# One backward-pass kernel: transposes issued one at a time, the order of the last convolution slices, and where the convolution ends

## The chip, the cores and the metric

The kernel runs on one core of a Trainium2 chip. The metric is the device time of one launch in microseconds (us); lower is better. The engines that matter here are TensorE (PE in the profile, with PEld for its weight loads), VectorE (DVE), ScalarE (ACT), GpSimd (POOL, which also issues DMAs) and SyncE (SP, whose queue issues most DMA loads). Each engine runs its instructions in the order in which they were built; engines wait for one another through semaphores.

## The reference

The kernel computes a forward pass and all its gradients. With `x` of 2048 rows and 1024 columns and `xn` its layer norm:

```python
s = A_ref(xn, k, v, shift_k, ssm_k, ssm_D)        # gated long convolution
g = silu(((xn @ w_gate) * (xn @ w_up)) @ w_down)  # bilinear unit, F = 3584
out = x + s * g

def A_ref(q, k, v, shift_k, ssm_k, ssm_D):
    kv = short_conv(k, shift_k, 4 taps) * v
    y = irfft(rfft(kv padded to 4096) * rfft(ssm_k padded))[:2048]
    return q * (y + kv * ssm_D)
```

The outputs are `out` and the gradients of x, k, v, the two convolution kernels, `ssm_D` and the three weights, for a given `grad_out`.

## The kernel before

The sequence is held as 16 row blocks of 128 rows. The first part of the kernel, on which the change works, is this:

- **Gate and up products.** F is cut into 14 slabs of 256 columns (`NSL`). A unit (`gu_unit`, L656) is one slab times four row blocks: per row block eight 128x512 matmuls into a tile `psg` (L671), then a ScalarE copy into `gut` (L673). When a unit's last row block is copied, VectorE multiplies the two halves into `hN` (`multiply`), and TensorE later transposes `hN` in four transposes of 32-bit pairs into a tile `tr` (`turn`, through `turn_pairs`, L205). ScalarE copies `tr` into `hT` (L699), which goes to DRAM (`HTd`). `defer` and `flush` put the transposes some row blocks later in the program; `flush()` without an age puts all that are left at once. The last two slabs are run half by half: first both slabs over row blocks 0 to 7, then both over 8 to 15. Between the halves stands `hn[0](); flush()` (L976 to L978), which puts the multiply and the four transposes of the newest unit right there.
- **The long convolution** (`conv_forward`, L709) runs beside these products. It works in eight slices of 128 columns. Per slice it transforms the kernel row (`h`, loaded, transposed by `h_rows`, then matmuls `psF` L242, ScalarE copies `SP`, VectorE sums into `KX`) and `kv` (into `HX`), multiplies the spectra (`product`), and takes the inverse: VectorE sums (`inv_dft` or `inv8`) followed by matmuls into `psY` in `tail`. `inv8`, with eight residues, makes VectorE do more sums and needs 16 `psY` matmuls (`inv8_rows`, L445); `inv_dft`, with four, needs 32 (`inv_rows`, L456). `INV8` lists the slices that take `inv8`: 2, 4 and 6. Slices 0 and 7 use a forward transform of eight residues (`EIGHT`).
- **Pacing.** The convolution is a generator whose yields give estimated VectorE time. `tick` (L941), called after each row block, advances it by `pump` in proportion to the rows done out of `NT` = 206. VectorE's instructions keep the program's order while `PIN` is set.
- **The down product.** `bm_mm` (L992) multiplies `HTd` rows by `w_down`: 56 matmuls of 128x512 per row block (L994). `bm_first` does row blocks 0 and 1 while the convolution's rest is ticked in; `drain()` puts what is left of the convolution. Then `gate` (L1212) treats each row block: four loads (`x_t`, `do_t`, `xn_t`, `yf_t`, two buffers each; `yf_t` is the convolution's stored result `YFd`), a ScalarE copy of the PSUM tile into `bm`, two sigmoids and eleven VectorE operations. The `w_down` factor's other operand `ht` is loaded for two row blocks at a time (`load_ht`): `ht1` and `ht2` early, the others from the row loop. All these loads go through SP's queue in its built order.

After that come the backward products, with the backward convolution on VectorE beside them; the change leaves them as they are.

Of the kernel before, what the change touches and what calls it, by code (L numbers as in the profile page):

```python
# [13 lines left out]
BF16 = mybir.dt.bfloat16  # L14
# [5 lines left out]
def build_kernel(  # L20
# [12 lines left out]
    P = 128  # L33
# [530 lines left out]
    def in_pairs(x):  # L564
        return x.bitcast(F32).rearrange("p (m q) -> p q m", q=4)

    def turn_row(i, x, q, qi):
        ps = ps_st.tile([P, 4, P], F32, name="tr")
        for dc in range(4):
            tr_ln[0] = turn_pairs(ps[:, dc, :], in_pairs(x)[:, dc])  # L570
        to = by_pair(XNT[q][:, :, qi * P:(qi + 1) * P])
        if i % 2 == 0:
            act_copy[0] = nc.scalar.copy(out=to, in_=halves_of(ps[:]))
        else:
            V.tensor_copy(to, halves_of(ps[:]))

    def layer_norm(b0, n, x4):
# [50 lines left out]
        c, r0 = divmod(b0, 8)  # L628
        return last, root, st(xnn[:, c, r0:r0 + n, :], x4[:, 0:n, :])

    def turn_late():
        for i, (x, q, qi) in enumerate(turn_rows):
            turn_row(i, x, q, qi)
        turn_rows.clear()

    nop = lambda: None
# [7 lines left out]
    def flush(age=0):  # L644

        for e in later:
            e[0] += 1
        while later and later[0][0] >= age:
            later.pop(0)[1]()

    turn_of = [0]
    hn = [nop]
    chunk = [0]

    def gu_unit(sl, b0, n, w, tick):

        if n == 4:
            turn_of[0] += 1
            if turn_of[0] % 3 == 0 and sl < NSL - 2:
                gut = U[5][:, 2048:4096].rearrange("p (a i f) -> p a i f", a=2, i=4)  # L660
            else:
                gut = fg.tile([P, 2, 4, SLW], BF16, name="gut")
            hN = fg.tile([P, 4, SLW], BF16, name="hN", bufs=3)
        else:
            gut = lnp.tile([P, 2, 2, SLW], BF16, name="gut_s", bufs=6)
            hN = lnp.tile([P, 2, SLW], BF16, name="hN_s", bufs=6)
        for i in range(n):
            q, qi = divmod(b0 + i, 4)
            ps = ps_gu.tile([P, 512], F32, name="psg")
            for dc in range(DC):  # L670
                gu_mm[0] = nc.tensor.matmul(ps[:], XNT[q][:, dc, qi * P:(qi + 1) * P],  # L671
                                            w[:, dc].rearrange("p a f -> p (a f)"), start=(dc == 0), stop=(dc == DC - 1))
            nc.scalar.copy(out=gut[:, :, i], in_=ps[:].rearrange("p (a f) -> p a f", a=2))  # L673
            flush(5)
            if i == 0:
                turn_late()
            hn[0]()
            hn[0] = nop
            tick()
        sta(GUd[sl, b0 // 8][:, :, b0 % 8:b0 % 8 + n], gut[:, :, 0:n])  # L680

        def multiply():
            with tc.issue_after(last.ins) if b0 + n <= 4 and chunk[0] <= 2 else nullcontext():
                tt(hN[:, 0:n], gut[:, 0, 0:n], gut[:, 1, 0:n], MUL)
            st(Hd[sl][:, b0:b0 + n, :], hN[:, 0:n])
            defer(turn)
        hn[0] = multiply

        def store(hT):
            fr, so = sl % 12 * SLW, b0 % 8 * P  # L690
            ld(HTd[b0 // 8][sl // 12][fr:fr + SLW, so:so + n * P].rearrange("(f a) s -> f a s", a=2),
               hT[:, :, 0:n].rearrange("f a i s -> f a (i s)"))

        def turn():
            hT = fg.tile([P, 2, 4, P], BF16, name="hT") if chunk[0] > 5 else lnp.tile([P, 2, 4, P], BF16, name="hT_s", bufs=5)
            ps = ps_tr.tile([P, 4, P], F32, name="tr")
            for i in range(n):
                turn_pairs(ps[:, i, :], hN[:, i, :].bitcast(F32))
            nc.scalar.copy(out=hT[:, :, 0:n].rearrange("f a i s -> f i a s"), in_=halves_of(ps[:, 0:n]))  # L699
            store(hT)  # L700

    h_out = []
    EIGHT = ((0, 0), (0, 1), (7, 0), (7, 1))
    INV8 = (2, 4, 6)
    SHIFT_W = 8 * 2.3

    conv_state = {"forward": True}
# [1 line left out]
    def conv_forward():  # L709
# [34 lines left out]
            yield 2.3  # L744

        def h_rows(ds, c):
            if ds == 8:
                return
# [8 lines left out]
            for r in range(1, 4):  # L757
                turn_pairs(ps[:, r, :], pairs[:, c, :, r])
# [66 lines left out]
        h_rows(0, 1)  # L825
        yield 0.1
        tl = turn_tables(ps_y)
        sp = [half(0, S_["hx"], i, Dz[:, 0:P]) for i in range(2)]
        for ds in range(8):
            yield 0.5  # L830
            if ds % 2 == 1 and ds < 7:
                with tc.issue_after(S_["kst"].ins):
                    for c in range(2):
                        load_kv(ds // 2 + 1, c)
            D0 = Dz[:, ds * P:(ds + 1) * P]
            sph = []
            KX = cx.tile([P, 16, 256], BF16, name="KX")
            HX = cs.tile([P, 16, 256], BF16, name="HX", bufs=2)
            own_room = lambda X: X[:].rearrange("p a x -> p (a x)").bitcast(F32).rearrange("p (a x) -> p a x", a=8)[:, 0:4]
            eight = (ds, 1) in EIGHT  # L840
            if ds == 0:
                yield from transform(0, 1, sp, HX, own_room(KX), lambda i: sph.append(half(0, kvs(0), i)), nop)
            else:
                yield from transform(ds, 0, sp, KX, own_room(HX), lambda i: sph.append(half(ds, S_["hx"], i, D0)), nop)
                S_["kst"] = st(KFd[ds], KX[:])
            next(tl, None)
            room = cf.tile([P, 4, 256], F32, name="room", tag="hx")[:] if eight else None
            yield from transform(ds, int(ds > 0), sph, HX if ds else KX, room, nop1 if eight else lambda c: h_rows(ds + 1, c),
                                 lambda: next(tl, None))
            if ds == 0:  # L850
                S_["kst"] = st(KFd[0], KX[:])
            if eight:
                h_rows(ds + 1, 0)
            turned(HX, 1, 0, 1)
            yield 1.3
            if eight:
                h_rows(ds + 1, 1)
            if ds == 7:
                cf.release()
                S_["forward"] = False  # L860
            st(HFd[ds], HX[:])
            yield from product(KX, HX, KX, cs, False, 0)
            if ds % 2 == 1 and ds < 7:
                yield from shift(ds // 2 + 1)
            sp = []

            def ahead():
                if ds < 7:
                    sp.append(half(ds + 1, kvs(ds + 1), len(sp)))
            yield from (inv8 if ds in INV8 else inv_dft)(KX, HX, cs, ahead if ds % 2 == 0 else None, ahead)  # L870
            if ds % 2 == 1:
                ahead()
            S_["G", ds] = HX
            tl = tail(ds)
        yield 6.0
        for _ in tl:
            yield 1.0
# [58 lines left out]
    ps_cv = pool("ps_cv", 2, space=PSUM)  # L936
    pump, drain = make_pump(conv, F_TOTAL)
    cnt = [-5]
    NT = 24 * 8.0 + 14

    def tick(by=1):  # L941
        cnt[0] += by
# [31 lines left out]
    for hf in range(2):  # L974
# [5 lines left out]
        for sl in range(NSL - 2, NSL):  # L980
# [4 lines left out]
                ld(HT0[1][:, 8:12], ht_rows(0, 24, 28))  # L985
            if (hf, sl) == (0, NSL - 2):

                assert len(h_out) == 8
                ld(HT0[1][:, 0:8], ht_rows(0, 16, 24))
    hn[0]()  # L990
# [218 lines left out]

    tr_name = ["tr"]  # L1210

    def gate(b, ps):  # L1212
# [10 lines left out]
        bm, sig, sgn, gg, so, dgg, ds_t = [T(n_) for n_ in ("bm", "sig", "sgn", "gg", "so", "dgg", "ds_t")]  # L1223
        dbm, dy, dxa, o_t = [O(n_) for n_ in ("dbm", "dy", "dxa", "o_t")]
        nc.scalar.copy(out=bm, in_=ps[:])
# [431 lines left out]
```

## Time and profile before

| what | value |
|---|---|
| three runs | 1934.62, 1935.11, 1936.25 us; median 1935.11 us |
| the profiled execution | 1935.74 us, of which the profile's span is 1934.0 us |
| PE busy | 1916.3 us of the span (99%) |
| DVE busy | 1554.1 us (80%) |
| ACT busy | 639.1 us (33%) |
| 50 to 450 us: PE, DVE busy of 400 | 395.45, 396.01 |
| 500 to 556 us: PE, DVE busy of 56 | 55.98, 34.05 |
| 556 to 700 us: PE, DVE busy of 144 | 144.00, 91.34 |

"Busy" is the union of an engine's instruction records, so a matmul's mean duration (380 ns for 128x512) is longer than the distance between two of them (216 ns). "Idle before" is what an engine lost ahead of an instruction, with the engine or DMA that ended the wait.

### The profile page before, as it was taken

To read this page: it belongs to the slowest core of one execution; us is meant where nothing else is said; L and a number is where in the kernel's file an instruction comes from. 1 tells how busy PE (TensorE), PEld (TensorE's weight loads), DVE (VectorE), ACT (ScalarE), POOL (GpSimd) and SP (SyncE) were. 2 spreads that over 40 slices of the span, in tenths; PEclk is the share of its full clock that TensorE was granted. 3 is DMA by queue.
4 is the path that set the end of the run, shared out by engine and by line. 5 is a ranking of instruction groups with operands and counts; after the bars stand their busy time and mean duration, and the time that the engine had idled before them with its cause. 6 is when DMAs were issued, how large, how long until landed. Compare 5 with 4: busy or idle time off the path is not lost.

```text
span 1934.0 us, 26795 instructions
## 1 busy us (share of the span) xinstructions
PE 1916.3 (99%) x10626; PEld 1033.6 (53%) x10626; DVE 1554.1 (80%) x1730; ACT 639.1 (33%) x942; POOL 320.6 (17%) x461
## 2 busy tenths in 40 slices
PE   8999999999999999999999999999999999999999
PEld 5555655555444447666666666664444444444444
DVE  9999999999937555888799999999996403488873
ACT  5855655555422224333222222222222102011122
POOL 4121212101112220000122122021121101111211
PEclk9999999999999999999999999999999999999999
DMA  8776866758789987666777788575797999899973
GB/s 281 258 256 228 255 221 217 222 212 287 239 253 319 312 272 266 211 217 202 256 250 256 246 243 276 188 268 194 210 260 172 146 216 201 181 186 192 194 205 118
DMA packets 451357, 444.38 MB, mean 230 GB/s; under 512 B 268800, under 2 KB 371612, under 8 KB 436768
## 3 DMA queue, kind: packets, MB, share of 16 engines
q1 hardware_dynamic: 394848, 243.36, 47.6%
q0 software_dynamic: 40064, 169.95, 27.5%
q10 hardware_dynamic: 16320, 29.36, 4.2%
q8 instruction: 83, 1.36, 0.3%
q14 instruction: 42, 0.34, 0.1%
HBM read 194.00 MB, written 185.64 MB: 196 GB/s over the span
## 4 chain that ended last, share of the span: by engine, by line
PE 84%; DVE 12%; issue 2%; DMA 1%; ACT 1%; SPq 0%; POOL 0%; DVEq 0%; ACTq 0%
PE psb L1365 20%; PE psx L1495 20%; PE psb L1348 10%; PE psbm L994 10%; PE psb L1443 9%; PE psg L671 9%; DVE W L220 3%; DVE KX L220 2%; PE psF L242 2%; DVE HX L220 2%; DVE U L220 2%; PE psY L445 1%; DVE hN L220 1%; PE tr L205 1%; DVE m L220 1%
## 5 line engine op out<-in xcount | busy, mean ns | idle before, releaser
L671 PE MATMUL psg<-wslab,U 128*128 128x512 bf16 x1792 | 409.7, 380 | 2.9 <-DMA wslab<-in_B_w_gate_dram 0.8
L1365 PE MATMUL psb<-U,U 128*128 128x512 bf16 x1792 | 397.1, 379 | 0.0
L1495 PE MATMUL psx<-U,dgut 128*128 128x512 bf16 x1536 | 332.8, 379 | 0.0
L1495 PEld LDWEIGHTS <-dgut 128*128 128x128 bf16 x1792 | 175.3, 98 | 211.4
L1365 PEld LDWEIGHTS <-U 128*128 128x128 bf16 x1792 | 175.2, 98 | 198.0
L671 PEld LDWEIGHTS <-U 128*128 128x128 bf16 x1792 | 175.7, 98 | 189.7 <-issue 4.7
L1348 PE MATMUL psb<-wdt,U 128*128 128x256 bf16 x1792 | 205.6, 273 | 0.0
L1348 PEld LDWEIGHTS <-U 128*128 128x128 bf16 x1792 | 175.3, 98 | 29.2
L1443 PE MATMUL psb<-U,U 128*128 128x512 bf16 x816 | 177.1, 379 | 0.0
L220 DVE TENSOR_TENSOR W<-W 128x1024 f32<-128x1024 f32 (+1 forms) x174 | 171.7, 1003 | 3.7
L1370 ACT CAST wb<-psb 128x512 bf16<-128x512 f32 x112 | 65.6, 586 | 315.4 <-PE psb L1365 310.5
L994 PE MATMUL psbm<-U,ht 128*128 128x512 bf16 x672 | 145.7, 379 | 0.0
L1443 PEld LDWEIGHTS <-U 128*128 128x128 bf16 x896 | 87.5, 98 | 104.5
L673 ACT CAST gut<-psg 128x512 bf16<-128x512 f32 x156 | 91.5, 587 | 125.2 <-PE psg L671 123.7
L1527 ACT ACTIVATE dx_t<-dxn 128x1024 bf16<-128x1024 f32 x15 | 15.9, 1057 | 324.2 <-DVE dxn L220 324.2
L994 PEld LDWEIGHTS <-ht 128*128 128x128 bf16 x672 | 65.6, 98 | 78.6
L220 DVE TENSOR_TENSOR U<-U,dht 128x2048 bf16<-128x2048 bf16 x56 | 68.3, 1222 | 46.3 <-ACT dht L1350 46.2
L1350 ACT CAST dht<-psb 128x512 bf16<-128x512 f32 x112 | 65.7, 587 | 116.3 <-PE psb L1348 115.2
L1193 DVE SCALAR_TENSOR_TENSOR dkp<-dkT,kT 128x1024 bf16<-128x1024 bf16 (+2 forms) x64 | 78.3, 1224 | 30.2 <-DMA dkT<-DKSHd 28.4
L220 DVE TENSOR_TENSOR dxn<-psx,dxna_t 128x1024 f32<-128x1024 f32 x15 | 18.3, 1222 | 86.5 <-PE psx L1495 82.6
L66 POOL DMA_DIRECT2D Hd<-hN x54 | 29.5, 547 | 294.1 <-DVE hN L220 285.6
L1474 ACT CAST wbs<-psb 128x512 bf16<-128x512 f32 x51 | 29.9, 586 | 145.3 <-PE psb L1443 134.0
(250 smaller groups left out, 2461.9 us busy)
## 6 DMA issues: line engine op xcount, KB each, us to landing
U<-GUd SPq DMA_DIRECT2D x28, 1024.0 KB, 8.0
DGd<-U SPq DMA_DIRECT2D x28, 1024.0 KB, 5.9
GUd<-gut ACTq DMA_DIRECT2D x39, 512.0 KB, 4.9
out_dram<-wb SPq DMA_DIRECT2D x112, 128.0 KB, 4.4
U<-Hd SPq DMA_DIRECT2D x14, 1024.0 KB, 6.6
Hd<-hN POOLq DMA_DIRECT2D x54, 256.0 KB, 4.2
HTd<-hT SPq DMA_DIRECT2D x52, 256.0 KB, 4.4
ht<-HTd SPq DMA_DIRECT2D x6, 1536.0 KB, 10.0
```

What stands on the lines that cost most here:

```text
L220: pinned(V.tensor_tensor(o, a, b, op))
L242: mm = nc.tensor.matmul(ps[:, k].rearrange("p (c d) -> p c d", c=2), T[:, r, k, :], xr[:, r], start=(n == 0), stop=(n == len(rs) - 1 and ( ...
L671: gu_mm[0] = nc.tensor.matmul(ps[:], XNT[q][:, dc, qi * P:(qi + 1) * P], w[:, dc].rearrange("p a f -> p (a f)"), start=(dc == 0), stop=(dc ...
L673: nc.scalar.copy(out=gut[:, :, i], in_=ps[:].rearrange("p (a f) -> p a f", a=2))
L994: mm = nc.tensor.matmul(ps[:, dh * 512:(dh + 1) * 512], ht(fc)[:, i * P:(i + 1) * P], WD[fc // 4][:, fc % 4, dh * 512:(dh + 1) * 512], sta ...
L1193: ins = V.scalar_tensor_tensor(prod[:].rearrange("p r d -> p (r d)")[:, lo:H], dkT[:, 0, lo:H], 1.0, kT[:, 0, 13 + m + lo:13 + m + H], op0 ...
L1348: nc.tensor.matmul(ps[:, x * SLW:(x + 1) * SLW], DBMT[2 * hf + g][:, dc, (b % 4) * P:(b % 4 + 1) * P], wdt[:, dc, :], start=(dc == 0), sto ...
L1350: nc.scalar.copy(out=dht[:, 2 * e:2 * e + 2].rearrange("p b f -> p (b f)"), in_=ps[:])
L1365: nc.tensor.matmul(ps[:], XN[b // 4][:, b % 4, dc * P:(dc + 1) * P], dgus[b // 8][:, :, b % 8], start=(b == 0), stop=(b == NB - 1))
L1370: nc.scalar.copy(out=wb[:, dc % 2].rearrange("p a f -> p (a f)"), in_=ps[:])
L1443: nc.tensor.matmul(ps, h[:, f, b, :], DBM[b // 4][:, b % 4, dh * 512:(dh + 1) * 512], start=(b == 0), stop=(b == NB - 1))
L1495: nc.tensor.matmul(ps[:, dh * 512:(dh + 1) * 512], t[n][:, f, i * P:(i + 1) * P], WGU[n][:, f, dh * 512:(dh + 1) * 512], start=(n == 0 and ...
```

## The change

The transposes become generators (`turn_row_steps`, `h_rows_steps`, and `turn` with a `yield`), kept in the lists `turns["h"]`, `turns["f"]` and `turns["rows"]`. After every gate/up matmul, `turn_step` may put one transpose into TensorE's order; `turn_out` puts all that are open when their result is due.

The convolution transforms slices 6 and 7 one after the other; the spectra of slice 6 are held (`held`), those of slice 7 use the room of `krow` (`late_room`), and then product and inverse follow for 6 and for 7. `INV8` gains slices 1 and 5. `NT` grows by 11 row blocks of ticks.

In the down product, row blocks 2 and 3 are multiplied, with ticks, before `drain()`; ScalarE copies their sums and those of 0 and 1 at once into `U[11]` (`bm_out`), and the four gates follow after the convolution. The row loop starts at row block 4.

```diff
+    def turn_step(left=99):
+        since[0] += 1
+        if open_[0] is None:
+            if turns["rows"] and left <= 4 * len(turns["rows"]):
+                open_[0] = turns["rows"].pop(0)[1]
+            elif since[0] > 10:
+                for kind in ("h", "f"):
+                    if turns[kind]:
+                        open_[0] = turns[kind].pop(0)[1]
+                        since[0] = 0
+                        break
+        if open_[0] is not None:
+            if next(open_[0], None) is None:
+                open_[0] = None
+            else:
+                since[0] = 0
...
@@ def flush
+        if age == 0:
+            turn_out("h", "f")
...
@@ def gu_unit
+        turn_out("h", before=mine - 2)
+        if b0 >= 8:
+            turn_out("rows")
...
+                turn_step(8 * (n - i) - dc)
             nc.scalar.copy(out=gut[:, :, i], in_=ps[:].rearrange("p (a f) -> p a f", a=2))
...
-            defer(turn)
+            defer(lambda: turns["h"].append((mine, turn())))
...
             for i in range(n):
+                if i > 0:
+                    yield 1
                 turn_pairs(ps[:, i, :], hN[:, i, :].bitcast(F32))
...
-    INV8 = (2, 4, 6)
+    INV8 = (1, 2, 4, 5, 6)
...
+        late_room = krow[:].rearrange("p c r x -> p (c r x)")[:, 0:4096].rearrange("p (a x) -> p a x", a=16)
...
-            KX = cx.tile([P, 16, 256], BF16, name="KX")
+            KX = cx.tile([P, 16, 256], BF16, name="KX")[:] if ds < 7 else late_room
...
+            if ds == 6:
+                held = (KX, HX)
+                continue
+            backs = [(ds, KX, HX)]
             if ds == 7:
                 cf.release()
                 S_["forward"] = False
-            st(HFd[ds], HX[:])
-            yield from product(KX, HX, KX, cs, False, 0)
...
+                backs.insert(0, (6, *held))
+            for e, KX, HX in backs:
+                for w in product(KX, HX, KX, cs, False, 0):
+                    if e == 7:
+                        next(tl, None)
+                    yield w
...
+                yield from (inv8 if e in INV8 else inv_dft)(KX, HX, cs, ahead if e % 2 == 0 else None, ahead)
...
-    NT = 24 * 8.0 + 14
+    NT = 24 * 8.0 + 25
...
+    def bm_out(b, ps):
+        bm = U[11][:, b * D:(b + 1) * D] if b < 4 else mt.tile([P, D], BF16, name="bm")[:]
+        nc.scalar.copy(out=bm, in_=ps[:])
+        return bm
...
     bm_first(range(4, NF))
+    early = [bm_out(b, pss[b]) for b in range(2)]
+    for b in (2, 3):
+        ps = (ps_bx if b == 2 else ps_bm).tile([P, D], F32, name="psbm")
+        for fc in range(NF):
+            bm_mm(ps, ht1[0], b - 2, fc)
+            if fc % 4 == 3:
+                tick(0.74)
+        early.append(bm_out(b, ps))
     drain()
...
-    for i in range(2):
-        gate(i, pss[i])
-    for bp in range(1, 8):
-        ht, ht_ld = load_ht(bp) if bp > 2 else (ht1, ht2)[bp - 1]
+    for b, bm in enumerate(early):
+        gate(b, bm)
+    for bp in range(2, 8):
+        ht, ht_ld = load_ht(bp) if bp > 2 else ht2
...
-            gate(2 * bp + i, ps)
+            gate(2 * bp + i, bm_out(2 * bp + i, ps))
```

More of the change, by code (lines that the diff above doesn't have):

```diff
@@ L565, in in_pairs, with turn_row, turn_row_steps @@
         return x.bitcast(F32).rearrange("p (m q) -> p q m", q=4)
-    def turn_row(i, x, q, qi):
+    def turn_row(*a):
+        run(turn_row_steps(*a))
+    def turn_row_steps(i, x, q, qi):
         ps = ps_st.tile([P, 4, P], F32, name="tr")
         for dc in range(4):
+            if dc > 0:
+                yield 1
             tr_ln[0] = turn_pairs(ps[:, dc, :], in_pairs(x)[:, dc])
@@ L629, in layer_norm, with turn_out @@
         return last, root, st(xnn[:, c, r0:r0 + n, :], x4[:, 0:n, :])
+    turns = {"h": [], "f": [], "rows": []}
+    open_ = [None]
+    since = [99]
+    def turn_step(left=99):
[14 more added lines that the diff above has]
+                since[0] = 0
+    def turn_out(*kinds, before=None):
+        if open_[0] is not None:
+            run(open_[0])
+            open_[0] = None
+            since[0] = 0
+        for kind in kinds:
+            while turns[kind] and (before is None or turns[kind][0][0] < before):
+                run(turns[kind].pop(0)[1])
+                since[0] = 0
     def turn_late():
         for i, (x, q, qi) in enumerate(turn_rows):
-            turn_row(i, x, q, qi)
+            turns["rows"].append((0, turn_row_steps(i, x, q, qi)))
         turn_rows.clear()
@@ L653, in build_kernel @@
     chunk = [0]
+    unit = [0]
     def gu_unit(sl, b0, n, w, tick):
+        unit[0] += 1
+        mine = unit[0]
+        turn_out("h", before=mine - 2)
+        if b0 >= 8:
+            turn_out("rows")
         if n == 4:
@@ L697, in turn @@
             for i in range(n):
+                if i > 0:
+                    yield 1
                 turn_pairs(ps[:, i, :], hN[:, i, :].bitcast(F32))
@@ L746, in h_rows, with hx_now, h_rows_steps @@
         def h_rows(ds, c):
-            if ds == 8:
-                return
+            if ds < 8:
+                turns["f"].append((0, h_rows_steps(ds, c)))
+        def hx_now():
+            turn_out("f")
+            return S_["hx"]
+        def h_rows_steps(ds, c):
             hrow = S_["h", ds]
@@ L757, in h_rows @@
             for r in range(1, 4):
+                yield 1
                 turn_pairs(ps[:, r, :], pairs[:, c, :, r])
@@ L827, in conv_forward @@
         tl = turn_tables(ps_y)
-        sp = [half(0, S_["hx"], i, Dz[:, 0:P]) for i in range(2)]
+        late_room = krow[:].rearrange("p c r x -> p (c r x)")[:, 0:4096].rearrange("p (a x) -> p a x", a=16)
+        sp = [half(0, hx_now(), i, Dz[:, 0:P]) for i in range(2)]
         for ds in range(8):
@@ L835, in conv_forward, with ahead, rows_and_next @@
             D0 = Dz[:, ds * P:(ds + 1) * P]
-            sph = []
-            KX = cx.tile([P, 16, 256], BF16, name="KX")
+            sph, ahead_sp = [], []
+            KX = cx.tile([P, 16, 256], BF16, name="KX")[:] if ds < 7 else late_room
             HX = cs.tile([P, 16, 256], BF16, name="HX", bufs=2)
-            own_room = lambda X: X[:].rearrange("p a x -> p (a x)").bitcast(F32).rearrange("p (a x) -> p a x", a=8)[:, 0:4]
+            own_room = lambda X: X.rearrange("p a x -> p (a x)").bitcast(F32).rearrange("p (a x) -> p a x", a=8)[:, 0:4]
             eight = (ds, 1) in EIGHT
+            def ahead():
+                if ds < 7:
+                    ahead_sp.append(half(ds + 1, kvs(ds + 1), len(ahead_sp)))
+            def rows_and_next(c):
+                h_rows(ds + 1, c)
+                if ds == 6:
+                    ahead()
             if ds == 0:
@@ L843, in conv_forward @@
             else:
-                yield from transform(ds, 0, sp, KX, own_room(HX), lambda i: sph.append(half(ds, S_["hx"], i, D0)), nop)
-                S_["kst"] = st(KFd[ds], KX[:])
+                yield from transform(ds, 0, sp, KX, own_room(HX[:]), lambda i: sph.append(half(ds, hx_now(), i, D0)), nop)
+                S_["kst"] = st(KFd[ds], KX)
             next(tl, None)
             room = cf.tile([P, 4, 256], F32, name="room", tag="hx")[:] if eight else None
-            yield from transform(ds, int(ds > 0), sph, HX if ds else KX, room, nop1 if eight else lambda c: h_rows(ds + 1, c),
+            yield from transform(ds, int(ds > 0), sph, HX if ds else KX, room, nop1 if eight else rows_and_next,
                                  lambda: next(tl, None))
             if ds == 0:
-                S_["kst"] = st(KFd[0], KX[:])
+                S_["kst"] = st(KFd[0], KX)
             if eight:
@@ L857, in conv_forward @@
                 h_rows(ds + 1, 1)
+            st(HFd[ds], HX[:])
+            sp = ahead_sp
+            if ds == 6:
+                held = (KX, HX)
+                continue
+            backs = [(ds, KX, HX)]
             if ds == 7:
@@ L860, in conv_forward @@
                 S_["forward"] = False
-            st(HFd[ds], HX[:])
-            yield from product(KX, HX, KX, cs, False, 0)
[L863 to L874, printed above, removed]
+                backs.insert(0, (6, *held))
[4 more added lines that the diff above has]
+                    yield w
+                if e % 2 == 1 and e < 7:
+                    yield from shift(e // 2 + 1)
+                yield from (inv8 if e in INV8 else inv_dft)(KX, HX, cs, ahead if e % 2 == 0 else None, ahead)
+                if e % 2 == 1:
+                    ahead()
+                S_["G", e] = HX
+                tl = tail(e)
         yield 6.0
@@ L986, in build_kernel @@
             if (hf, sl) == (0, NSL - 2):
+                turn_out("f")
                 assert len(h_out) == 8
@@ L1210, in build_kernel, with gate @@
     tr_name = ["tr"]
-    def gate(b, ps):
+    def bm_out(b, ps):
+        bm = U[11][:, b * D:(b + 1) * D] if b < 4 else mt.tile([P, D], BF16, name="bm")[:]
+        nc.scalar.copy(out=bm, in_=ps[:])
+        return bm
+    def gate(b, bm):
         c, r = divmod(b, 8)
@@ L1222, in gate @@
         O = lambda nm_: mo.tile([P, D], BF16, name=nm_)[:]
-        bm, sig, sgn, gg, so, dgg, ds_t = [T(n_) for n_ in ("bm", "sig", "sgn", "gg", "so", "dgg", "ds_t")]
+        sig, sgn, gg, so, dgg, ds_t = [T(n_) for n_ in ("sig", "sgn", "gg", "so", "dgg", "ds_t")]
         dbm, dy, dxa, o_t = [O(n_) for n_ in ("dbm", "dy", "dxa", "o_t")]
-        nc.scalar.copy(out=bm, in_=ps[:])
         nc.scalar.activation(sig, bm, ACT.Sigmoid)
```

## The prediction

> **What bounds the kernel now.** First the page's busy shares with the slices of the span (40 slices of 48.4 us, busy tenths).
>
> ```profile
> PE 1916.3 (99%) x10626; PEld 1033.6 (53%) x10626; DVE 1554.1 (80%) x1730; ACT 639.1 (33%) x942; POOL 320.6 (17%) x461
> ...
> PE   8999999999999999999999999999999999999999
> ...
> DVE  9999999999937555888799999999996403488873
> ```
>
> TensorE (PE) is full everywhere, but in the first ten slices VectorE (DVE) is just as full: two engines at their limit, and any point where the one must wait for the other in order shows who is behind. The stage table (length; busy us of PE, PEld, DVE, ACT, POOL; PE clock; DMA share; GB/s) and the list of PE's waits show that point.
>
> ```profile
> 50.00:450.00 400.00, 395.45 (x2254) 224.17 (x2253) 396.01 (x353) 236.37 (x328) 66.96 (x103) 1.00 0.70 232
> 450.00:500.00 50.00, 46.15 (x236) 24.17 (x235) 49.41 (x56) 26.54 (x38) 3.78 (x7) 0.93 0.93 307
> 500.00:556.00 56.00, 55.98 (x287) 28.12 (x286) 34.05 (x36) 15.37 (x24) 3.86 (x6) 1.00 0.77 226
> ```
>
> ```profile
> PE tr L205 <- DVE hN L220: 3.8, 1, 3.8
> ```
>
> PE's longest wait of the whole span is one transpose of `hN`, in the only stage between 50 us and the end in which the clock is below 1. The timeline of the two engines there (start, length):
>
> ```profile
> 483.55 0.69 DVE L220 TENSOR_TENSOR hN<-gut 128x1024 bf16<-128x1024 bf16 x1
> ...
> 491.75 0.69 DVE L220 TENSOR_TENSOR hN<-gut 128x1024 bf16<-128x1024 bf16 x1
> ```
>
> ```profile
> 487.53 1.24 PE L671 MATMUL psg<-wslab,U 128*128 128x512 bf16 x5
> 492.58 1.09 PE L205 MATMUL tr<-ident,hN 128*128 128x128 f32 x4 [3.81 <-DVE hN L220]
> 493.47 4.72 PE L671 MATMUL psg<-wslab,U 128*128 128x512 bf16 x11
> ```
>
> This is the `flush()` between the halves of the last two slabs (I call it the boundary). The multiply stands behind convolution work in DVE's order, PE stands behind the multiply. So **the time at which PE passes the boundary, 492.58, is DVE's time, not PE's.** The price is more than the wait: at PE's granted clock by stretches,
>
> ```profile
> 488.00:491.00 3.00, 0.77 (x4) 1.00 0.69 154
> 491.00:495.00 4.00, 2.42 (x8) 0.51 1.04 371
> 495.00:498.00 3.00, 3.00 (x8) 0.52 1.02 408
> ```
>
> the clock is halved for some 7 us. From 492.58 to 498.03 PE does 4 transposes and 11 matmuls, worth 4 x 0.109 + 11 x 0.216 = 2.8 us at full clock (distances between starts elsewhere), in 5.45: 2.6 us lost.
>
> **The change, part by part.**
>
> *VectorE work ahead of the boundary multiply.* I count it in the two built orders, with distances between starts (a little under the durations, since neighbours overlap: two of 0.69 take 1.29). Leaving, because slice 6 is only transformed there: its product (one 128x4096 at 2.2; four pairs of 128x2048 at 2.27, 2.52, 2.52, 2.28: 11.8) and its eight-residue inverse (two `W<-KX` 2.32, four `W<-W` 1.26, four `HX<-W` 0.60, two `W<-W` of 512 0.61, four L290 0.60: 15.7). Entering: slices 1 and 5 change from a four-residue inverse (2 x 2.32 + 4 x 1.14 = 9.2) to 15.7, 2 x 6.5 = 13.0; and slice 7's transform has got further (four sums 4.6, two of 1.26, two L290: 8.3). Net -27.5 + 13.0 + 8.3 = **-6.2 us**. DVE's idle time up to there (some 6 us, half of it before 30 us) I leave as it is: its reasons, loads and the norm at the start, are not touched. PE passes the boundary at 492.58 - 6.2 = 486.4.
>
> *Does PE get there sooner?* Its arrival before is 492.58 - 3.81 = 488.77. Two inverses lose 32 `psY` matmuls at 0.109: 3.5 us. Single transposes: a group of four runs in 0.43 start to start, as four singles would; five groups that waited for the one `tr` buffer cost more:
>
> ```profile
> 33.70 0.27 PE L205 MATMUL tr<-ident,hN_s 128*128 128x128 f32 x1
> 33.80 1.67 PE L671 MATMUL psg<-wslab,U 128*128 128x512 bf16 x7
> ```
>
> ```profile
> 107.88 0.60 PE L205 MATMUL tr<-ident,hN 128*128 128x128 f32 x4
> ...
> 109.63 0.75 PE L205 MATMUL tr<-ident,U 128*128 128x128 f32 x4
> ```
>
> The lone transpose of the first two lines takes 0.10 to the next matmul: no dearer than a grouped one. The group at 109.63 starts 0.24 late (five matmuls from 108.31 end at 109.39) and takes 0.15 more; over the five groups 1.6 us. The price of 247 singles (6 before) is thus between -2 and +0.7 us (3 ns each); I take -1.6. PE arrives at 488.77 - 5.1 = 483.7 and **waits 2.7 us** (1.3 to 4.4 with these bounds). So the saved PE work and the single transposes are worth nothing: the wait covers them, and if DVE were early, they would show, 5.1 us at most.
>
> *The clock.* A wait of 3.8 cost 2.6 us; one of 1.3 at 52.73 cost nothing. 2.7 lies between: 0 or 2.6. Of the 3.8 us only about 2.5 lay before the clock fell at 491, and few waits of 2.7 would lie as well in one such stretch; I take 0, so 2.6 us are won, and keep 2.6 as a bound.
>
> The Trainium skill ("TensorE: Matmul & The Clock Gate", Part 1) has free-running windows of 3.4 us, of which an idle one halves the clock, and advises against idle gaps of 3 us; by it a wait of 2.7 leaves the clock up, the sum below as it stands, and the 3.8 us here agrees with it.
>
> *Behind the boundary.* PE's work is the same (the eight-residue `psY` of slice 6 and the 32 of slice 7 lay there before too), row blocks 2 and 3 are the same 112 matmuls earlier, their `ht1` is the load issued at 536.77 ahead of all gates: 0. DVE's extra work (60 us of convolution left at 486.4, so done near 547) goes into the stage where it has 22 us idle; slice 7's `psY` comes up on PE about 565 (first down matmul 486.4 + 28, 224 matmuls at 0.216), 18 us later. Without that cover PE would wait. Four gates at once take DVE 4 x 6.7 us; the next PSUM tile that depends on them is wanted at row block 8, some 9 us after it is free.
>
> *A new wait.* Gates now begin after the last `psY`, which stands 236 matmuls into the down product, 100 before row block 6 needs the third `ht`. Before:
>
> ```profile
> 555.34 1.04 PE L456 MATMUL psY<-HX,TI 128*128 128x256 bf16 x8
> ...
> 562.72 0.33 SPq L61 DMA_DIRECT2D yf_t<-YFd  x1
> ...
> 565.04 0.38 SPq L61 DMA_DIRECT2D ht<-HTd  x1
> ```
>
> ```profile
> ht<-HTd SPq DMA_DIRECT2D x1, 1536.0 KB, 13.0
> ```
>
> The last `psY` ends at t = 556.38, the store of `YFd` lands, `yf_t` is loaded, gate 0's `so` runs at 565.43 = t + 9.05. This `ht` was issued at t + 8.7 and landed 13.0 us later, 24 us ahead of use (row block 6 at 602). In the changed SP order it stands behind three loads of gate 2, which wait until gate 0 has read its first buffers (`dxa`, three operations after `so`): t + 9.05 + 3 x 0.61 + 0.69 + 0.4 = t + 12.0. The other early `ht` loads took 10.0, 12.7 and 9.0. Row block 6 comes at t + 100 x 0.216 - 0.2 = t + 21.4. The wait is 12.0 + 10.0 - 21.4 = 0.6 by the median of all six, 3.6 by the one in this place, 0 by the shortest. I take the mean of the first two, **2.1 us**; behind it in PE's order stand the down product's row blocks and all that follows, so it counts in full. The second piece, behind gate 1 (t + 20.5, 9.3 us), lands before its use at t + 32.
>
> **Sum**: -6.2 - 2.6 + 2.1 = -6.7 us. The profiled execution took 1935.74 for its span of 1934.0; the median is 1935.11. Taken off the median: 1928.4, with 0 to 3.6 for `ht` 1926.3 to 1929.9. A run of this kernel tells 0.2% (3.9 us) from no change: faster is below 1931.2, slower above 1939.0.
>
> **Rivals.**
> 1. *The clock falls at the boundary all the same.* For it: the wait is still 2.7, up to 4.4. Then -6.2 + 2.1: 1931.0 (1928.9 to 1932.5).
> 2. *The wait for `ht` takes over*, at its long end and with a fallen clock: -6.2 - 2.6 + 3.6 + 2.6 = -2.6: 1932.5. For it: the 13.0 at this very place; against: that load shared the DMAs with five gate loads, this one with three.
> 3. *DVE does not get ahead*: kernel-row transposes, now single and queued behind those of `hN`, come late, DVE idles for `SP`, and the 6.2 us go there: about 1934.6 with the clock kept as before plus `ht`, 1937.2. Against it: such waits of DVE are under 1 us in all now.
> 4. *Slower: each single transpose exposes the weight load of the matmul behind it*, 0.098 us, all along the gate/up products: 241 x 0.098 = 23.6 us; PE reaches the boundary at 507.3, is itself the bound, and passes at 508.3: +15.7 - 2.6 + 2.1 = +15.2, 1950.3. It decides from 55 ns each (13.3 us, where the boundary's gain is gone and 3.9 more). Against it: the pair at 33.70. The skill ("TensorE: Matmul & The Clock Gate", Weight-path perf modes) speaks for it: 32-bit weights get no fast load. The 32-bit loads are longer here too (142 ns against 98), and exposing 44 ns 241 times would make 10.6 us, no gain at all.
>
> **How the numbers follow.** Forecast 0.50, rival 1 0.22, rival 2 0.14, rival 3 0.07, rival 4 0.07. Faster: all of the first, some 0.13 of rival 1 and 0.03 of rival 2: 0.66. Slower: rival 4, 0.03 of rival 3, 0.01 of rival 2 with both clock losses: 0.11. The rest, 0.23, is within 0.2%. The range 1925.5 to 1933.0 leaves out rivals 3 and 4 and the end of rival 2; its low end adds 0.8 for waits that I count as unchanged.
>
> **What the profile after would show.** The wait `PE tr <- DVE hN` near 486 at 1 to 4 us (right: PE passes within a microsecond of 486.4), clock 1.00 around it or not (rival 1); a wait of `psbm` for DMA `ht` at about 595, absent before; 176 instead of 208 `psY` matmuls from `HX`; distances after single transposes of 0.11 (rival 4: more). A boundary passed later than 489 would break the count of VectorE's work, and a wait for `psY` near 565 the cover behind it.

## The result, and the profile after

The changed kernel takes 1949.3 us (median of 4 runs, 1942.6 to 1952.0) against 1934.86 us for the kernel before (4 runs, 1934.12 to 1936.25): ratio 1.0061, interval 1.0038 to 1.0084 (the medians alone give 1.0075). It is **slower by 0.4 to 0.8%**, where 0.2% can be told. The forecast was 1928.4 us and faster. The profiled execution took 1952.0 us for its span of 1950.1; it is the longest of the four, so the balance below is that of a long one.

Where the time went is read in three steps. First the list of TensorE's waits in the changed kernel (engine, line, what it waited for; us in all, times, longest):

```profile
PE tr L1324 <- DVE dbm L220: 10.6, 2, 5.6
PE psbm L1067 <- DMA ht<-HTd: 6.2, 2, 3.8
PE tr L205 <- DVE hN L220: 3.0, 1, 3.0
```

Before, the third was 3.8 and the first two were not there. TensorE's timeline places them (start, length, idle time before it and its releaser):

```profile
486.25 1.08 PE L205 MATMUL tr<-ident,hN 128*128 128x128 f32 x4 [3.02 <-DVE hN L220]
...
598.66 13.51 PE L1067 MATMUL psbm<-U,ht 128*128 128x512 bf16 x53 [3.83 <-DMA ht<-HTd]
...
675.18 20.46 PE L1067 MATMUL psbm<-U,ht 128*128 128x512 bf16 x92 [2.37 <-DMA ht<-HTd]
...
700.62 1.03 PE L1324 MATMUL tr<-ident,dbm 128*128 128x128 bf16 x8 [4.98 <-DVE dbm L220]
...
733.42 1.03 PE L1324 MATMUL tr<-ident,dbm 128*128 128x128 bf16 x8 [5.59 <-DVE dbm L220]
```

TensorE passes the boundary at 486.25 instead of 492.58, 6.3 us sooner, and then loses everything in the row loop of the down product. Its end is the copy of row block 15's sums on ScalarE, here from the timeline of before and then of after:

```profile
724.44 1.01 ACT L1225 CAST bm<-psbm 128x1024 bf16<-128x1024 f32 x1 [2.92 <-PE psbm L994]
```

```profile
740.62 1.01 ACT L1287 CAST bm<-psbm 128x1024 bf16<-128x1024 f32 x1 [5.12 <-PE psbm L1067]
```

16.2 us later. What follows is unchanged: 1934.0 - 724.4 = 1209.6 us to the end of the span before, 1950.1 - 740.6 = 1209.5 after. So the whole result lies between 486 and 741 us, and it can be balanced: from the boundary to that copy 231.9 us before and 254.4 after, 22.5 more. The four waits above, without the boundary's, make 16.8. The rest is the clock: it is at half in the records from 486.2 to 489.6, 598.8 to 602.2, 697.8 to 704.6 and 732.0 to 738.8, of which TensorE was at work for 16.1 us (8.05 lost); before, 5.3 us of work were at half (2.65 lost). 16.8 + 5.4 is 22.2 of the 22.5. With -6.3 at the boundary that gives the 16.2.

Second, why are `ht` and `dbm` late? The stage table of before, then of after (length; busy us of PE, PEld, DVE, ACT, POOL; PE clock; share of the 16 DMA engines; GB/s):

```profile
556.00:580.00 24.00, 24.00 (x115) 10.98 (x113) 13.69 (x22) 11.04 (x11) 6.19 (x9) 1.00 0.87 274
...
600.00:620.00 20.00, 20.00 (x94) 9.11 (x93) 16.37 (x27) 6.03 (x6) 5.72 (x9) 1.00 1.09 331
```

```profile
556.00:580.00 24.00, 23.90 (x127) 12.41 (x128) 2.68 (x4) 6.67 (x9) 1.12 (x1) 1.00 0.18 55
...
600.00:620.00 20.00, 19.95 (x88) 8.79 (x88) 9.62 (x16) 2.93 (x3) 5.04 (x8) 0.94 1.10 361
```

The row loop is a stage that the DMAs fill: in slices of 20 us from 600 to 700 us their share is 0.99 to 1.12 before and 1.07 to 1.14 after. From 700 to 720 us it falls to 0.60 before, while it is 1.21 after. In the changed kernel they lie nearly idle for the 24 us ahead of the stage, and VectorE with them (2.68 us of 24), because the gates wait for the convolution's last `psY`, which now comes 17 us later (573.0 instead of 556.1). Gate 0's `so`, the first operation that needs `yf_t`, from VectorE's timeline after (565.43 before):

```profile
583.39 0.69 DVE L220 TENSOR_TENSOR so<-xn_t,yf_t 128x1024 bf16<-128x1024 bf16 x1 [3.61 <-DMA yf_t<-YFd]
```

From there to the end of gate 15's `dbm` it takes 747.2 - 583.4 = 164 us, before 731.0 - 565.4 = 166. These two lengths alone say little, because gate 15 waits for TensorE's row block 15 in both. VectorE's own waits in the stage say more, before and then after (the longest of each `gg` line, 23.4 and 27.3 us, lies ahead of gate 0):

```profile
DVE gg L220 <- ACT sig L1226: 70.8, 11, 23.4
DVE so L220 <- DMA yf_t<-YFd: 12.2, 4, 6.8
```

```profile
DVE so L220 <- DMA yf_t<-YFd: 45.5, 9, 12.5
DVE gg L220 <- ACT sig L1303: 38.9, 3, 27.3
```

Before, the gates mostly waited for TensorE's row blocks (through ScalarE's `sig`), and from gate 8 on no gate waited for a load. After, they wait for `yf_t`, gates 8 to 14 for 31.6 us of the 45.5. They start 18 us later and go at the pace of their loads; TensorE, ahead by 6, runs into them.

Third, where does it run into it? SP's queue before (one line) and after, at the third transposing load of `DBMd` (start, length on the queue):

```profile
688.58 3.96 SPq L1297 DMA_TRANSPOSE U<-DBMd  x1
```

```profile
699.18 17.68 SPq L1382 DMA_TRANSPOSE U<-DBMd  x1
717.27 0.34 SPq L61 DMA_DIRECT2D do_t<-in_grad_out_dram  x1
...
718.25 0.49 SPq L61 DMA_DIRECT2D yf_t<-YFd  x1
```

The load holds SP for 17.7 us instead of 4.0, and the loads of gate 14 stand behind it; VectorE waits 12.55 us for that `yf_t` until 727.60, and TensorE for gate 14's `dbm` until 733.4. Gate 12's `yf_t` stands in the same way behind two transposing loads of `w_down`, which hold SP for 7.8 and 5.6 us: issued at 688.6, it lets VectorE wait 8.25 us, and TensorE waits for that `dbm` until 700.6.

### The profile page after: what moved, and what is told of

The parts are those of the page before. It is cut to its first block, busy times and chain, and to the rows that moved or that the text cites. A ratio compares the mean times of both kernels' runs of the same rounds, so it can differ in the third digit from the quotient of the medians.

```text
span 1950.1 us, 26629 instructions
## 1 busy us (share of the span) xinstructions
PE 1909.1 (98%) x10465; PEld 1040.0 (53%) x10594; DVE 1566.4 (80%) x1750; ACT 639.5 (33%) x942; POOL 321.4 (16%) x461
## 4 chain that ended last, share of the span: by engine, by line
PE 62%; issue 0%; ACT 0%; DVE 0%; ACTq 0%
PE psb L1450 20%; PE psx L1580 20%; PE psb L1433 10%; PE psb L1528 9%; PE psY L1214 1%; PE psY L445 1%; PE psx L1528 1%; PE psF L242 1%; PE psbm L1067 0%; PE psY L1528 0%; ACT B L302 0%; PE tr L1324 0%; DVE dbm L220 0%; ACT wbs L1675 0%; ACT wb L1455 0%
## 5 line engine op out<-in xcount | busy, mean ns | idle before, releaser
L718 PE MATMUL psg<-wslab,U 128*128 128x512 bf16 x1739 | 420.3, 380 | 4.3 <-DMA wslab<-in_B_w_gate_dram 0.9
L220 DVE TENSOR_TENSOR W<-W 128x1024 f32<-128x1024 f32 (+1 forms) x186 | 184.0, 1005 | 4.1
L1067 PE MATMUL psbm<-U,ht 128*128 128x512 bf16 x658 | 150.8, 389 | 6.9 <-DMA ht<-HTd 6.2
L220 DVE TENSOR_TENSOR W<-SP 128x1024 f32<-128x1024 f32 x64 | 74.3, 1220 | 0.7
```

The source lines that it names most:

```text
L220: pinned(V.tensor_tensor(o, a, b, op))
L1067: mm = nc.tensor.matmul(ps[:, dh * 512:(dh + 1) * 512], ht(fc)[:, i * P:(i + 1) * P], WD[fc // 4][:, fc % 4, dh * 512:(dh + 1) * 512], sta ...
```

## The experiments

Fourteen kernels, in four rounds. Ratios are to the kernel before in the same session, with their intervals.

**Round 1: which part costs the time?** `gates_early` takes the down-product part back:

```diff
...
-    early = [bm_out(b, pss[b]) for b in range(2)]
-    for b in (2, 3):
...
     drain()
...
-    for b, bm in enumerate(early):
-        gate(b, bm)
-    for bp in range(2, 8):
+    for i in range(2):
+        gate(i, bm_out(i, pss[i]))
+    for bp in range(1, 8):
```

> The changed kernel with one part undone: the convolution is drained, and gates 0 and 1 are built, right behind row blocks 0 and 1 of the down product, as before; row blocks 2 and 3 are back in the row loop. Transposes, slice order, inverses and pace stay. The last psY then stands 148 matmuls into the down product instead of 236, 19 us earlier at 0.216 each. Theory 'late gates' (sixteen gates form one chain of loads and VectorE work that took 164 us before and after, so a later start ends the stage later): the first so runs near 565 instead of 583, PE does not wait for dbm or only little, 1928 to 1934 us. Rival 'transposes or inverses' (the loss comes from another part): the time stays above 1944 with the waits for dbm gone or not.

`late_only` puts that part (with `bm_out`, and `NT = 24 * 8.0 + 18`) into the kernel before.

> The kernel before with only this part of the change: row blocks 2 and 3 multiplied with ticks ahead of the drain, their sums copied early, pace NT 210 instead of 206; grouped transposes, three inverses of eight, slices in order. The last psY stands at 184 matmuls instead of 124. VectorE has 5.1 us less ahead of the boundary (by the built order), so PE passes it near 488.8 with little or no wait, 4 to 6 us earlier than before. Theory 'late gates': the gates start about 13 us later into the down product, net some 7 us later than 565, and the stage ends later by as much: PE waits for dbm near 700 to 735, 1936 to 1945 us. Rival 'the start of the gates is free': the gain at the boundary stays whole, 1928 to 1931 us.

`inv3` has `INV8 = (2, 4, 6)` in the changed kernel.

> The changed kernel with inverses of eight residues in slices 2, 4 and 6 alone, as before. VectorE has 10.6 us less ahead of the boundary (by the built order), PE 3.5 us more. Theory 'late gates': PE passes the boundary near 486.7 without a wait and with the clock up, all else stays late, 1942 to 1952 us, no more than 3 us from the changed kernel. Rival 'VectorE's added work of the two inverses sets the loss': the time falls to 1938 or below.

`grouped` runs the transposes' generators at once:

```diff
-            defer(lambda: turns["h"].append((mine, turn())))
+            defer(lambda: run(turn()))
...
-                turns["f"].append((0, h_rows_steps(ds, c)))
+                run(h_rows_steps(ds, c))
```

> The changed kernel with every transposition of four put out at once again instead of one at a time. Theory 'late gates': no difference beyond the spread of the changed kernel, 1942 to 1952 us. Rival 'each single transpose exposes a weight load': 10 us or more faster, and the distance from a single transpose to the next matmul is above 0.15 us in the changed kernel's trace.

| kernel | median us (range) | ratio, interval | first `so` | row block 15 copied |
|---|---|---|---|---|
| gates_early | 1937.38 (1931.33 to 1944.53) | 1.0010, 0.9993 to 1.0027 | 568.4 | 732.4 |
| late_only | 1948.89 (1941.54 to 1952.54) | 1.0059, 1.0039 to 1.0079 | 571.6 | 737.6 |
| inv3 | 1949.01 (1948.02 to 1954.69) | 1.0073, 1.0055 to 1.0091 | 586.7 | 737.3 |
| grouped | 1951.56 (1945.53 to 1956.19) | 1.0088, 1.0065 to 1.0111 | 585.7 | 733.8 |

The one part makes the whole net loss: alone it costs what the whole change costs, 4 us above the range expected of it, and without it no loss can be told. The gain is gone without it too: `gates_early` passes the boundary at 486.49, 6 us sooner, and gives this back further on. `inv3` and `grouped` stay where the changed kernel is. In `late_only` TensorE waits only 0.4 us at the boundary, as expected, and then these two in its list of waits:

```profile
PE tr L1251 <- DVE dbm L220: 9.4, 1, 9.4
PE psbm L994 <- DMA ht<-HTd: 7.5, 2, 4.2
```

A start of the gates only 6.2 us later than before, with a TensorE that passes the boundary 2.2 us sooner (490.38), is enough. `gates_early` missed its expectation by some 3 us at the median, and its single runs lie 13 us apart. Its profile, of a long one, lists:

```profile
PE tr L1324 <- DVE dbm L220: 8.4, 1, 8.4
PE psY L456 <- DVE HX L220: 3.0, 1, 3.0
```

The second of them is at the `psY` of the convolution's last inverse, which row blocks 2 and 3 cover in the changed kernel. The third transposing load held SP for 17.0 us there too. `inv3` missed its expectation at the boundary, which TensorE passed at 491.85 and not near 486.7: with VectorE early, it waited 3.9 us near 480 for a ScalarE copy, and the clock fell. This counts below.

**Round 2: the transposing load, or the traffic?** `after_no_q2` drops the load and lets TensorE transpose row blocks 8 to 11; `before_no_q2` and `early_no_q2` (on `gates_early`) have the same edit.

```diff
-        if b >= 12:
+        if b >= 8:
             defer(turn)
...
-        if bp in (3, 5, 7):
+        if bp in (3, 5):
```

> The changed kernel, but the third transposing load (U from DBMd, row blocks 8 to 11) is left out and TensorE transposes these four row blocks of dbm as it does 12 to 15: some 1.8 us more on TensorE (four times eight transposes, 0.46 us each set in the changed kernel's trace). Theory 'slow transposing load' (SP is held 17.7 us by it, the loads of gates 14 and 15 stand behind it): the waits for dbm near 700 and 733 shrink to 2 us or less in all, those for ht (6.2 us) stay, 1936 to 1942 us. Rival 'the sixteen gates are bound by the amount of DMA traffic': the time falls by 3 us at most, 1945 to 1951 us.

> The kernel before with the same edit, as a control. In its trace this load took 6 us and nobody waited. Both theories: 1.8 us slower from the transposes, 1935 to 1938 us; by 'slow transposing load' its single executions above 1940 should be gone.

> gates_early with the same edit. Theory 'slow transposing load': its executions, 1931 to 1945 us with the load, come together, without the wait for dbm (8.4 us in its profile): 1930 to 1935 us. Rival 'amount of traffic': the spread stays, median 1936 to 1939 us.

`after_q2_last` issues the load after the row loop, ordered behind gate 15's `yf_t`.

> The changed kernel with the third transposing load behind the loads of gates 14 and 15 in SP's queue. Theory 'SP's order' (these loads are late because they stand behind it): the waits for dbm fall to 3 us or less, 1936 to 1944 us, unless the load itself is late for its reader near 740. Rival 'DMA engines shared' (the order in the queue does not matter): within 3 us of the changed kernel.

| kernel | median us (range) | ratio, interval |
|---|---|---|
| after_no_q2 | 1947.50 (1944.57 to 1950.20) | 1.0069, 1.0052 to 1.0086 |
| before_no_q2 | 1937.27 (1936.40 to 1938.16) | 1.0014, 1.0004 to 1.0023 |
| early_no_q2 | 1936.25 (1933.63 to 1941.58) | 1.0006, 0.9997 to 1.0016 |
| after_q2_last | 1943.89 (1938.79 to 1947.41) | 1.0043, 1.0029 to 1.0058 |

The theory that blamed this load fell. Without it TensorE waits 5.3 us for `ht` at 598 and 5.7 us for `dbm` at 651.5, where the first of its new transposes meets the gates: **the wait moved to the next place where TensorE needs a gate.** By the medians the edit gains 1.8 us on the changed kernel, by the ratios nothing; with its own price set against it (2.2 us in the control) the load accounts for 4 of the 14 us at most. On `gates_early` the same edit takes the wait for `dbm` out of the profile, but only 1.1 us off the median, and the single runs still lie 8 us apart. The load's place in the queue matters about as much: `after_q2_last` is 5 us faster by the medians, at the far end of what was expected of SP's order, and its interval overlaps that of the changed kernel. Its wait for `dbm` did not fall to 3 us as expected; it is 7.2 us, now at gate 12 (702.6). The load is one way in which the lateness shows, not its source.

**Round 3: traffic by itself; the predicted wait; a version without the loss.** `after_half_loads`:

```diff
-        for nm_, src in (("x_t", xq[:, c, r, :]), ("do_t", gout[:, c, r, :]), ("xn_t", xnn[:, c, r, :]), ("yf_t", YFd[:, b, :])):
+        for nm_, src in (("xn_t", xnn[:, c, r, :]), ("yf_t", YFd[:, b, :])):
...
-        x_t, do_t, xn_t, yf_t = ins
+        xn_t, yf_t = ins
+        x_t, do_t = xn_t, yf_t
```

> The changed kernel with half of the gates' loads left out: x_t and do_t are not loaded, xn_t and yf_t are used in their place, so `out` and the gradients that come from them are other numbers; all order, all VectorE and TensorE work and the late start of the gates stay. It takes 16 times 0.5 MB off SP's queue between 570 and 740 us. Theory 'late gates meet a stage that the DMAs fill' (share of the 16 engines 1.0 to 1.15 there): the waits for dbm (10.6 us) and at least the second wait for ht go, 1928 to 1937 us. Rival 'the late start itself, by VectorE's 107 us of gates and the order of the loads': waits for dbm remain, 1943 us or more.

`after_ht_first` calls `load_ht(3)` ahead of the gates, with gate 2's loads ordered behind it.

> The changed kernel with the third load of ht (both pieces) ahead of the loads of gate 0 in SP's queue. The wait of 3.8 us at row block 6, the one the prediction named, goes with its fallen clock. Theory 'late gates': the first gates start some 5 us later behind 1.75 MB, and the waits for dbm at the end grow by about as much: 1945 to 1952 us, no gain that can be told. Rival 'each wait stands for itself': 5 us faster than the changed kernel, 1941 to 1946 us.

`both_early` is `gates_early` with `INV8 = (2, 4, 6)` and `NT = 24 * 8.0 + 20`; `both_early_grouped` adds the edit of `grouped`.

> A version that takes the gain and leaves the loss: the changed kernel with the gates started behind row blocks 0 and 1 as before, inverses of eight in 2, 4 and 6 alone as before, and a pace NT of 212 (206 before, 217 changed). By the built order VectorE has 10.5 us less than before ahead of the boundary (4.3 less than the changed kernel), so TensorE sets the time there, near 485 unless a store of hT holds ScalarE as it did in inv3, and the last psY stands at 124 matmuls of the down product as in before. Theory 'late gates': all that follows keeps its distance from the boundary, so 1925 to 1930 us. Rival 'the gain at the boundary is always given back by the DMAs behind it': 1933 us or more.

> The same version with transposes put out in fours at once. Here no wait for VectorE covers TensorE's work ahead of the boundary, so the price of single transposes shows: by the prediction's step 1.6 us slower than both_early (bounds: 2 slower to 0.7 faster); by rival 4 of the prediction, 10 us or more faster.

| kernel | median us (range) | ratio, interval |
|---|---|---|
| after_half_loads | 1936.84 (1933.75 to 1944.35) | 1.0002, 0.9988 to 1.0016 |
| after_ht_first | 1958.16 (1955.12 to 1963.93) | 1.0112, 1.0087 to 1.0137 |
| both_early | 1935.58 (1934.08 to 1942.77) | 1.0002, 0.9989 to 1.0014 |
| both_early_grouped | 1935.91 (1933.85 to 1939.09) | 0.9998, 0.9986 to 1.0009 |

`after_half_loads` leaves out half of the gates' loads: 8 MB less in the row loop, and the loss is gone, with all order and the late start kept (`so` at 582.4). In the kernel before, TensorE has no wait in this stage that fewer loads could take away. Its list of TensorE's waits:

```profile
PE tr L1325 <- DVE dbm L220: 5.7, 1, 5.7
...
PE psbm L1067 <- DMA ht<-HTd: 0.7, 1, 0.7
```

The waits for `ht` are nearly gone, those for `dbm` halved, and from `so` of gate 0 to the end of gate 15's `dbm` it takes 150 us instead of 164: the loads are most of it, not all. The edit takes bytes off the DMA engines and 32 issues off SP's queue at once; it does not tell which of the two counts. `after_ht_first` is the sharpest answer. It removes the very wait that the prediction priced, and is 9 us slower than the changed kernel, above the range of either theory: the gates start later still (`so` at 589.0), and TensorE waits 5.1, 7.7 and 7.2 us further on. In this full stage the transfer that was put ahead delayed the others.

`both_early` got rid of both late gates and VectorE's wait, and still gained nothing: TensorE passes the boundary at 495.01 and row block 15 is copied at 724.3, where it was before. (Its profiled execution is a long one, 1940.1 us, but what it has more comes later.) TensorE's timeline and SP's queue there:

```profile
483.59 6.15 PE L718 MATMUL psg<-wslab,U 128*128 128x512 bf16 x17 [6.59 <-ACT gut L721]
```

```profile
461.56 22.03 SPq L61 DMA_DIRECT2D HTd<-hT  x3
```

ScalarE waited 8.65 us for a store of `hT`, and SP spent 22 us on three such stores, behind 1.5 MB of `ht` and 2 MB of `w_down`. So a second limit, the DMAs ahead of the boundary, lies just under the one that VectorE set; round 4 tests this.

**Round 4: is the gain real if the DMAs are not full?** `both_early_wd` moves one load of 1 MB; `before_wd` is the kernel before with that move alone.

```diff
         load_wd(0)
-        load_wd(1)
...
             flush()
+            load_wd(1)
             load_wd(2)
```

> both_early, where TensorE waited 6.6 us at 483.6 for a copy of ScalarE that stood behind a store of hT (SP spent 22 us on three of these stores, behind 1.5 MB of ht and 2 MB of w_down). Here the second w_down load (1 MB) comes after the boundary. Theory 'DMA traffic ahead of the boundary gives the gain back': the wait is 3 us or less, the gain of some 6 us shows, 1926 to 1932 us. Rival 'it comes back further on': the wait goes but the time stays, 1934 us or more.

> Control: the kernel before with that load moved alone. Its boundary waits for VectorE (3.8 us at 492.6), so by both theories no change: 1934 to 1937 us.

`both_early_wd`: 1930.35 us (1926.72 to 1936.76), ratio **0.9978, interval 0.9970 to 0.9987**: it beats both kernels. `before_wd`: 1935.62 us, 1.0003 (0.9994 to 1.0012). In the first, the same views read:

```profile
486.05 0.64 PE L205 MATMUL tr<-ident,hN 128*128 128x128 f32 x4
```

```profile
460.59 15.62 SPq L61 DMA_DIRECT2D HTd<-hT  x3
```

TensorE passes the boundary at 486.05 without a wait, the clock does not fall once up to the end of the span, and row block 15 is copied at 715.4, 9 us sooner than before. Its profiled execution is the shortest of the twelve; the median gains 4 us, and the third transposing load still took 10.7 us on SP in it. What makes single runs differ by 10 us was not settled.

## Why the prediction was wrong

- **The boundary was right.** VectorE is busy for 478.4 us up to there instead of 484.5, 6.1 us less (forecast 6.2), and idle for 7.8 instead of 8.1 (I had read some 6). TensorE passes at 486.25, forecast 486.4. TensorE's arrival: 486.25 - 3.02 = 483.2, forecast 483.7; the wait 3.0, forecast 2.7.
- **Single transposes and the two inverses were said to be worth nothing behind that wait**: only in part tested. Grouped, TensorE arrives at 488.0 - 2.6 = 485.4, so singles bring 2.2 us there (forecast 1.6), and 2.1 in `both_early` against its grouped form, where a longer wait takes it. In `grouped` VectorE comes later too: TensorE passes at 488.02, 1.8 us after the changed kernel, and VectorE idles 10.4 us up to 488 instead of 7.8. By this one trace singles help VectorE a little; no total shows it. Rival 4, the slower case that I named, did not happen: `grouped` is no faster, and from a single transpose to the next matmul it takes 0.11 us (504.76 to 504.87, after). That rival 4's 1950.3 us lies near the result is chance.
- **The clock was mis-sized.** I took a wait of 2.7 us as free. After 3.02 us it fell for 3.4 us, from 486.2: 1.7 us lost, so the won part of the 2.6 is 0.9. This is rival 1 with a smaller price; the last section works out why the wait was not free.
- **The first wait for `ht` was the right mechanism, a little long.** This `ht` was issued 13.0 us behind the last `psY` (forecast 12.0), took 12.1 us to land (forecast 10.0), and TensorE waited 3.83 (forecast 2.1, bound 3.6). The fallen clock behind it, which only rival 2 had, cost 1.7 more (3.4 us of work at half from 598.8).
- **The step that failed is "Behind the boundary", and the last lines of "A new wait".** I followed the 18 us delay of `psY` for as far as the next PSUM tile, at row block 8, and the next two `ht` pieces, and let the gates' later start cost 0 beyond that. The runs showed in its place sixteen gates whose loads the full DMAs held back, so that the late start was not made up: 2.37 + 4.98 + 5.59 us of waits in the other row blocks and, with the two falls at 697.8 and 732.0, 4.7 us of clock: 17.6 us that no term and no rival held. The profile of before had a sign of it, DMA shares up to 1.12 in the stage. My stage table showed the share only up to 556 us, and I read it for TensorE.
- **The gain would also have been smaller than its sum.** That VectorE sets the boundary was true, but what is bound next there is the DMAs, not TensorE: `both_early` shows the second limit, `both_early_wd` the gain when it is out of the way.

Shown by runs: that the down-product part makes the net loss (`gates_early`, `late_only`), and that the gates' loads in the row loop carry most of it (`after_half_loads`). Only argued: that within the part it is the gates' late start, and not the two row blocks or the early copies that come with it; and how the loss divides between the DMA engines, the order of SP's queue and VectorE's own 107 us of gates.

## What to carry to other kernels

When work is moved later, ask for the chain behind it when its last link is due, not its first: compare the chain's length with the time that is left, in the stage where it runs. Here a stage with the DMA share at 1 did not make up a late start, though VectorE was busy for only some 60% of it, and a transfer put ahead only passed its delay on. And when a wait is removed, look at which limit is next in the same place before the gain is counted.

## What the hardware showed

- **The transposing load slows down threefold in company.** Of the third `DBMd` load I counted the 4096 packets of 256 bytes: mean 18 ns each before, 60 ns after, 72 ns in `gates_early`; from issue to landing 6.0, 25.5 and 28.9 us. The DMA view over the stretch of these packets, before and after:

```profile
DMA packets 4124, 1.06 MB, mean 259 GB/s; under 512 B 4116, under 2 KB 4116, under 8 KB 4124
```

```profile
DMA packets 4553, 2.48 MB, mean 135 GB/s; under 512 B 4190, under 2 KB 4190, under 8 KB 4552
```

  Before, the load has the engines for itself; after, the gates' stores lie among it, and all of it together moves at half the rate. The Trainium skill ("DMA: Bandwidth & Descriptors", Latency and other measured facts) gives 261 GB/s for transposing loads with a non-contiguous middle dimension, measured on one kernel, and some 350 to 400 GB/s for contiguous ones. The 259 GB/s of the first line agree with the lower figure, the 135 of the second with neither.
- **A wait need not fill a clock window to cost one.** Waits of 3.0 us were followed by 3.4 us at half clock (486.2, and 548.7 in `gates_early`), one of 2.35 us too (`inv3` at 601.2); one of 2.37 us was not (after, 675.2), nor one of 3.36 us (`grouped`, 600.0). What decides can be counted from the falls themselves. In each trace they start whole steps of 3.41 us apart (in the changed kernel 486.19, 598.83, 697.82, 731.95: 33, 62 and 72 steps from the first). In the step ahead of each of the 32 falls of all traces TensorE was busy for at most 38%: 0.45 us of 3.41 from 482.78 (after), 1.06 from 598.08 (`inv3`), and the most, 1.31, from 485.92 (`grouped`). In every step at full clock with no fall behind it, from 20 to 1900 us of the span, it was busy for at least 44%: the least is 1.49 us from 630.81 (`late_only`), and in `grouped` 1.51 from 595.14, where the end of a step at 598.55 splits the wait of 3.36 us. The limit lies between, and so it is the place of a wait among the steps, with its length, that sets its price. The Trainium skill ("TensorE: Matmul & The Clock Gate", Part 1) says that a window of about 3.4 us runs freely and that the clock falls after an idle one. The steps agree with the first; for the second, a step that was 38% busy was enough here.
